# Seven block products with a PSUM tile each, and plain products for the first columns of each layer

## The chip, the cores and the metric

One core of a Trainium2 chip runs the whole program. The time is device microseconds (us) of one execution. Beside the timed executions one was taken by the hardware profiler; its trace is where all rows below come from.

## What is computed

Capped attention for 4 batches of 12 heads (448 rows, head size 64), then two feed-forward layers over the 1792 x 768 result, all in float32:

```python
scores = cap * np.tanh(scale * (q @ k.T) / cap)
attn = np.exp(scores - np.max(scores, axis=-1, keepdims=True))
x = (attn / (np.sum(attn, axis=-1, keepdims=True) + 1e-09)) @ v      # heads joined to 768 columns
h = np.maximum(x @ w_in, 0.0)          # layer 1: 768 -> 2048 -> 768
x = h * h @ w_out
g = x @ w_gate                         # layer 2: 768 -> 1536 -> 768
y = (g * (1.0 / (1.0 + np.exp(-g)))) * (x @ w_val) @ w_out2
```

## The kernel before

**Two passes.** Pass 0 computes the attention of batches 0 and 1, then the two layers for them, with the attention of batches 2 and 3 spread over its matmuls (12 pairs of heads, each opened by a gate at a certain matmul). Pass 1 computes the two layers for batches 2 and 3. Every float32 operand is split into two float32r parts, a high one (a cast on ScalarE) and a low one (a subtraction on VectorE), and a product is three matmuls (high x high, high x low, low x high) of 128 x 128 weights with 448 columns.

**Units of pass 1.** `pairs()` lists them: "1s" and "2s" are blocks that compute two columns of 128 of the hidden layer for both batches at once, "1b" and "2b" multiply the hidden layer by the second matrix in groups of FG = 4 columns (12 units of 12 matmuls in a group). A block takes two output columns, the two batches and the two halves of the 768 inputs as a 2 x 2 matrix of blocks and forms the product from seven block products instead of eight (the Strassen and Winograd scheme): 7 x 3 x 3 = 63 matmuls where plain ones need 72. There are 20 blocks: 8 in layer 1 (two ahead of each of its four groups), 12 in layer 2 (four ahead of each of its three).

**Operands of a block.** Four are the activations' quarters, named "11", "21", "12" and "22" (first digit: half of the inputs; second: batch 2 or 3), of three 128-row chunks c each. "12" is not an operand itself. Four sums T1 to T4 come from them (`SUMS`, `x_sum`, L579 to L582), and each operand is split by `o_hi` (ScalarE, L589) and `o_lo` (VectorE, L593). In layer 1 the quarters are read back from a DRAM copy, xhold (`x_back`, L572), in rounds by c, as their buffers have one or two places: T1 to T3 first (`BACK`), then again for "11", "21", "22" and T4 (`AGAIN`, which waits for the last T3). A last store into xhold follows the last attention pair's `norm` (L385). In layer 2 the quarters are the running sums of `gather` (L731).

**Products and PSUM.** `SEVEN` gives the seven products p0 to p6 in order; `s_mm` (L612) issues them. PSUM has eight places of 512 float32 columns: two for tag f0, two for f1, and a two-sided tile each for tags "s" and "a". p0 and p1 take f0, p4 takes f1; p2 and p3 are the two sides of one "s" tile, p5 and p6 the two sides of one "a" tile. `s_sum` reads them: p0 on ScalarE (L619), on VectorE u from p2 (L622), v from p3 (L625), w from p5 (L627), and the four results cs (L631) from p1, p4, p5 and p6. `unit_mm` (L682) issues all other products.

**Order.** The `Plan` class simulates the engines with fixed durations and writes one order for every engine from it; each step has a rank, which decides between steps that could start at the same time. AHEAD, LATER, FIRST, LAST, EARLIER and the like are parts of ranks or gates. Engines then work in that order; waits between engines follow from which tiles an instruction reads and writes.

Of the kernel before, what the change touches and what calls it, by code (L numbers as in the profile page):

```python
# [101 lines left out]
def kernel(  # L102
# [34 lines left out]
    FIRST = [15.0, 5]  # L137
    LAST = [80.7, 37.1]
    STRETCH = 2.1
    EARLIER = 16.02  # L140
    LEAD = 21.46
    BYC = 6.75
    BYK = 1.6

    AHEAD = dict(
        ld=28.6, lv=9.7, tr=8.5, cp=1.8, sc=9.4, th=-2.8, top=-8.4, par=14.9, mp=6.1, sub=21.2,
        ex=19.3, rs=-6.5, av=31.2, rc=15.1, norm=-38.3, xh=32.2, xl=26.8,
    )
# [4 lines left out]
    PACE = 7.11
    SLACK = 2.39
    MARGIN = 0.21
    DECODE = 77.14
# [402 lines left out]
    KINDS = ("11", "21", "T2", "T1", "22", "T3", "T4")  # L559
# [3 lines left out]
    for c in range(3):  # L563
        xo["11", c], xo["21", c], xo["T4", c], xo["22", c] = xbuf[0][c], xbuf[0][c + 3], xbuf[1][c], xbuf[1][c + 3]
# [26 lines left out]
    def o_lo(kind, c):  # L591
# [5 lines left out]
    SEVEN = ((0, 0, "11", "f0", 0), (0, 1, "21", "f0", 0), (2, 1, "T2", "s", 0), (2, 0, "T1", "s", 1),  # L597
             (3, 0, "22", "f1", 0), (1, 0, "T3", "a", 0), (1, 1, "T4", "a", 1))
    bank, u_t, c_t = {}, {}, {}

    def s_mm(i, p, c):
        k, half, kind, tag, side = SEVEN[p]
# [104 lines left out]
    def gate_m(i, b):  # L707
        sg = tmp_t[i, b] = fp.tile([P, S], F32, tag="sg", bufs=2, name="sg")
        V.scalar_tensor_tensor(sg, r_t.pop((i, b)), 1.0, ffn_ps.pop((i, b))[:, :S], ALU.add, ALU.mult)
# [124 lines left out]
    PAIR = 6.41  # L834
# [3 lines left out]
    for ps, (bs, seq) in enumerate(passes):  # L838
        order = [(i, b) for i, u in enumerate(seq) for b in bs[:: -1 if ps else 1] if b == bs[0] or not seven(u)]
        if ps == 0:  # L840
            order = [(i, b) for b in bs for i in range(NPRE)] + order[NPRE * len(bs) :]
        lens = [MM3 * (21 if seven(seq[i]) else cnt(seq[i])) for i, _ in order]
        heads, spent, at = 0, 0.0, t
        room = sum(lens) - FIRST[0] - LAST[0]
        late = B * KD - EARLY * KD
        for n, (i, b) in enumerate(order):
            if ps == 0 and heads < late and spent >= FIRST[0] + room * heads / (late - 1) - 1e-6:
                gates[EARLY * KD + heads] = steps[-1], t
                heads += 1
# [74 lines left out]
    def x_users(kind, c):  # L924
        return [("xt", 2, t, c) for t, two in SUMS.items() if kind in two] + [("xo", 2, kind, c)] * (kind in KINDS)
# [4 lines left out]
    for stage in (1, 2):  # L930
        for c in range(3):
            at = start_t[1, units7["12"[stage - 1]][0], 2] - 24 + BYC * c

            free_x = [("mm", 0, gone, b, x) for b in range(2) for x in (c, c + 3)]
            if stage == 1:
                for n, (kind, tag, bufs, to) in enumerate(BACK):
                    b, p = x_where(kind, c)
                    add(("xr", kind, c), "SP", (0.4, 0.6), at + n - EARLIER, x_back, (kind, c, tag, bufs),
                        [("hold", b * KD + p), ("norm", B * KD - 1)], [("rb" if tag == "r" else tag, bufs, [("xt", 1, t, c) for t in to])])
                for n, (kind, tag, bufs) in enumerate(AGAIN):  # L940
                    b, p = x_where(kind, c)
                    add(("xw", kind, c), "SP", (0.4, 0.6), at + n, x_back, (kind, c, tag, bufs), [("hold", b * KD + p), ("xt", 1, "T3", 2)],
                        [("rb" if tag == "r" else tag, bufs, [("xo", 1, kind, c)] + [("xt", 1, "T4", c)] * (kind == "21"))])
# [9 lines left out]
            for n, (kind, (one, two)) in enumerate(SUMS.items()):  # L953
                fourth = kind == "T4"
# [8 lines left out]
                add(("xt", stage, kind, c), "DVE", DVE1 * (1 + fourth), at + 4 + BYK * n - EARLIER * (stage == 1 and not fourth), summed, (kind, c), deps,  # L963
                    [("xt", 2, [("xo", stage, kind, c)] + [("xt", stage, "T2", c)] * (kind == "T1"))])
            for n, kind in enumerate(KINDS):
                ring = []
                if stage == 2:
                    deps = [src(kind), ("sm", last1, PART[kind], c)]
                elif (kind, c) in HOME:
                    deps = [src(kind)]  # L970
                    tag = HOME[kind, c]
                    ring = [(tag, RING[tag], [("sm", last2, PART[kind], 2)])]
                else:
                    deps = [src(kind) if kind in SUMS else ("xw", kind, c)] + free_x
# [5 lines left out]

                early = EARLIER * (stage == 1 and (kind, c) in HOME)
                add(("xi", stage, kind, c), "ACT", ACT1, at + 5 + BYK * n - early, high, (kind, c), deps, ring)
                add(("xo", stage, kind, c), "DVE", DVE1, at + 6 + BYK * n - early, o_lo, (kind, c), [("xi", stage, kind, c)])

    def plan_seven(i, t, prev):
# [3 lines left out]
        for p, (y, _, kind, tag, side) in enumerate(SEVEN):  # L989
            for c in range(3):  # L990
# [39 lines left out]
    for ps, (bs, seq) in enumerate(passes):  # L1030
        prev, before, when = None, {}, {}
        for ps_, i, b, t in [s for s in steps if s[0] == ps]:
# [5 lines left out]
            if ps and (i, b, 0) not in when:  # L1038
# [12 lines left out]
            for c in range(n):  # L1051
                deps = [("wl", ps, i)] if c == 0 else [K("mm", c - 1)] if ps == 0 else []
                if ps:
                    deps.append(before[i, b, c])
                if u[0] == "1a":
                    deps.append(("xl", b * KD + c))
# [6 lines left out]
                if c == 0 and u[0] == "1a" and not ahead:  # L1063
                    deps.append(("xl", b * KD + KD - 1))
# [11 lines left out]
            if ups(u):  # L1076
                used = [("mm", ps, m, b, u[1] % FG) for m, w in enumerate(seq) if not ups(w) and w[0][0] == u[0][0] and w[1] == u[1] // FG]
                G_ = ("g", GB, used)
# [5 lines left out]
            elif u[0] == "2a" and u[2] == 0:  # L1084
                add(K("gt"), "ACT", ACT1, end, gate_t, (i, b), [K("mm", n - 1)], [("r", 2, [K("gm")])])
                add(K("gm"), "DVE", DVE1, end + 0.5, gate_m, (i, b), [K("gt")], [("sg", 2, [("val", ps, i + 1, b)])])
# [5 lines left out]
            else:  # L1092
# [10 lines left out]
                add(K("ga"), "DVE" if g else "ACT", DVE1 if g else ACT1, end, gather, (i, b, e, g == 0), deps, ring)  # L1103
# [51 lines left out]
```

## Time and profile before

| | us |
|---|---|
| median of 3 runs | 1256.6 (1256.52 to 1257.73) |
| profiled execution, its own time | 1251.19 |
| its span, first to last instruction | 1249.1 |
| TensorE (PE) busy in the span | 1196.1 |
| VectorE (DVE) busy | 980.9 |
| ScalarE (ACT) busy | 577.6 |

The page of the profile gives busy times, the span in 40 slices with the granted clock of TensorE, the chain of work that ended last and the costliest groups of instructions. Matmuls overlap, so that their mean duration is longer than the distance between their starts, and a busy PE is not a PE at its peak.

### The profile page before, as it was taken

Reading aid. Unit: us, or ns where it says so; the run is one execution under the profiler, and the core shown is the slowest. Engines: PE = TensorE matmul, PEld = TensorE weight load, DVE = VectorE, ACT = ScalarE, POOL = GpSimd, SP = SyncE. Lnnn points to the kernel's source line nnn. Section 1 sums busy time; section 2 is a strip of 40 time slices with the busy share of each in tenths; the row PEclk is TensorE's granted clock in tenths of the full one; section 3 lists DMA queues with packets and bytes.
Section 4 is the critical chain, followed back from the end, with each engine's and each line's share of the span. In section 5 each row is a group of like instructions: output and inputs, shape, how many; then the busy total and the mean of one; then the engine's idle time right before and its main releaser. Section 6 shows DMA issues by size and latency. Waiting matters only on the chain.

```text
span 1249.1 us, 16273 instructions
## 1 busy us (share of the span) xinstructions
PE 1196.1 (96%) x6112; PEld 965.8 (77%) x6112; DVE 980.9 (79%) x1589; ACT 577.6 (46%) x886; POOL 73.3 (6%) x31
## 2 busy tenths in 40 slices
PE   8989999999999999999999979989899899999997
PEld 5334487887887887888788858878787798888887
DVE  5999888888888989888898987465646986576774
ACT  6998664635354343444224246452525444332330
POOL 2232110100000001010000000000000000000000
PEclk9999999999999999999999979999999899999999
DMA  7252068455554654744754754121212112111114
GB/s 139 68 135 67 16 170 225 113 152 165 153 142 126 170 162 126 217 128 131 191 150 135 201 154 125 53 68 40 64 33 68 50 35 81 49 54 64 43 34 89
DMA packets 215295, 136.93 MB, mean 110 GB/s; under 512 B 144912, under 2 KB 194224, under 8 KB 215216
## 3 DMA queue, kind: packets, MB, share of 16 engines
q1 hardware_dynamic: 213360, 135.66, 39.8%
q8 instruction: 48, 0.79, 0.3%
q10 hardware_dynamic: 1856, 0.23, 0.1%
q14 instruction: 31, 0.25, 0.1%
HBM read 100.86 MB, written 35.00 MB: 109 GB/s over the span
## 4 chain that ended last, share of the span: by engine, by line
PE 88%; DVE 8%; DMA 1%; issue 1%; ACT 1%; SPq 0%; POOL 0%; DVEq 0%
PE ff L682 55%; PE ff L612 21%; PE av L349 5%; PE sc L263 5%; DVE mx L282 1%; PE rs L313 1%; DVE te L300 1%; DVE cs L631 1%; DMA out_dram<-ob 1%; PE rs L333 0%; DVE acc L731 0%; DVE u L622 0%; DVE x L593 0%; DVE xt L582 0%; DVE u L627 0%
## 5 line engine op out<-in xcount | busy, mean ns | idle before, releaser
L682 PE MATMUL ff<-g,wp 128*128 128x448 f32 x2016 | 416.6, 367 | 2.9 <-DVE acc L731 2.1
L682 PEld LDWEIGHTS ff<-g,wp 128*128 128x128 f32 x2016 | 378.0, 188 | 42.9 <-issue 8.8
L682 PE MATMUL ff<-x,wp 128*128 128x448 f32 x1440 | 301.9, 368 | 0.0
L682 PEld LDWEIGHTS ff<-x,wp 128*128 128x128 f32 x1440 | 267.8, 188 | 41.4 <-issue 19.2
L612 PE MATMUL ff<-x,wp 128*128 128x448 f32 x720 | 165.3, 376 | 24.8 <-DVE cs L631 10.0
L612 PEld LDWEIGHTS ff<-x,wp 128*128 128x128 f32 x720 | 135.6, 192 | 46.8 <-DVE cs L631 15.3
L508 ACT CAST wp<-wx 128x512 fp32r<-128x512 f32 (+1 forms) x124 | 85.0, 687 | 124.3 <-DVE wx L490 79.3
L612 PE MATMUL ff<-xo,wp 128*128 128x448 f32 x540 | 120.6, 372 | 5.7 <-DVE u L622 5.7
L731 DVE TENSOR_TENSOR acc<-ff,acc 128x448 f32<-128x448 f32 x120 | 74.3, 622 | 59.1 <-PE ff L682 58.5
L612 PEld LDWEIGHTS ff<-xo,wp 128*128 128x128 f32 x540 | 102.7, 191 | 17.4 <-DVE u L622 8.7
L287 POOL PARTITION_ALL_REDUCE mr<-mx x24 | 72.5, 3023 | 587.0 <-DVE mx L282 544.1
L513 DVE TENSOR_TENSOR wp<-wx,wp 128x512 fp32r<-128x512 f32 (+1 forms) x124 | 95.8, 776 | 12.2 <-ACT wp L508 11.8
L263 PE MATMUL sc<-kT 64*112 64x448 f32 x384 | 86.9, 563 | 1.8 <-DVE kT L245 1.2
L631 DVE TENSOR_TENSOR cs<-ff,u 128x448 f32<-128x448 f32 x80 | 49.6, 621 | 37.2 <-PE ff L612 36.7
L304 ACT ACTIVATE tt<-tt,capt 112x896 f32<-112x896 f32 x60 | 62.4, 1046 | 21.5 <-DVE tt L300 21.4
L490 DVE SCALAR_TENSOR_TENSOR wx<-wr,wx 128x512 int32<-128x512 int32 (+1 forms) x82 | 68.2, 832 | 1.3
L488 DVE SCALAR_TENSOR_TENSOR wx<-wr,wx 128x512 int32<-128x512 int32 (+1 forms) x82 | 67.1, 818 | 1.6
L547 ACT CAST wp<-wx 128x768 fp32r<-128x768 f32 x40 | 33.4, 836 | 65.4 <-PE ff L682 46.3
L263 PEld LDWEIGHTS sc<-kT 64*112 64x112 f32 x384 | 30.5, 172 | 42.1 <-issue 25.8
L276 ACT ACTIVATE tt<-sc,capt 112x896 f32<-112x896 f32 x48 | 45.9, 1005 | 35.7 <-PE sc L263 35.6
L552 DVE TENSOR_TENSOR wp<-wx,wp 128x768 fp32r<-128x768 f32 x40 | 38.1, 953 | 25.2 <-ACT wp L547 25.1
L547 ACT CAST wp<-ws 128x384 fp32r<-128x384 f32 x60 | 29.0, 512 | 59.6 <-PE ff L612 30.2
(94 smaller groups left out, 1195.1 us busy)
## 6 DMA issues: line engine op xcount, KB each, us to landing
w<-wx SPq DMA_DIRECT2D x40, 384.0 KB, 2.8
wx<-w SPq DMA_DIRECT2D x40, 384.0 KB, 3.1
wr<-in_moe_w_in_dram SPq DMA_DIRECT2D x16, 768.0 KB, 5.7
wr<-in_moe_w_out_dram SPq DMA_DIRECT2D x24, 512.0 KB, 4.0
w<-wx SPq DMA_DIRECT2D x42, 256.0 KB, 2.3
wx<-w SPq DMA_DIRECT2D x42, 256.0 KB, 2.6
wr<-in_moe_w_gate_dram SPq DMA_DIRECT2D x12, 768.0 KB, 5.1
wr<-in_moe_w_val_dram SPq DMA_DIRECT2D x12, 768.0 KB, 5.3
```

Source lines behind the costliest of these rows:

```text
L263: PE.matmul(to, d["kT"][r, 0, c * CP : (c + 1) * CP], d["kT"][r, 1], start=True, stop=True)
L287: G.partition_all_reduce(d["m"].rearrange("p j s -> p (j s)"), d["mx"].rearrange("p j s -> p (j s)"), CP, bass_isa.ReduceOp.max)
L304: A.activation(t, t, AF.Exp, scale=c_abs)
L349: PE.matmul(d["av"][64 * j : 64 * j + 64, :S], d["v"][:, j, c], d["t", c][:, j], start=(c == 0), stop=(c == NC - 1),)
L488: V.scalar_tensor_tensor(x, hi, -0x40000000, x, ALU.bitwise_and, ALU.bitwise_or)
L490: V.scalar_tensor_tensor(x, lo, 29, x, ALU.logical_shift_right, ALU.bitwise_or)
L508: A.copy(piece((ps, i), n)[:, 0, :m], raws[1, i, i % 2] if ps else raws[0, i])
L513: V.tensor_tensor(hl[:, 1, :m], raws[1, i, i % 2] if ps else raws[0, i], f32(hl[:, 0, :m]), ALU.subtract)
L547: A.copy(t[:, 0, r], src)
L612: PE.matmul(bank[i, p], hl[:, h, 3 * half + c], x[:, t], start=(c == 0 and n == 0), stop=(c == 2 and n == 2))
L682: PE.matmul(ffn_ps[i, b][:, :S], hl[:, h, c], x[:, t], start=(c == 0 and s == 0), stop=(c == cnt(u) - 1 and s == 2),)
L731: V.tensor_tensor(acc, pt, acc, ALU.add)
```

## The change

Each of the seven products gets a PSUM tile of its own: p0 and p4 take f0, p1 and p5 f1, p2 the "s" tile, p3 and p6 the "a" tile one after the other. Of "s" and "a" only one side is then used. In layer 1 the first two hidden columns, in layer 2 the first (its gate and its value), are computed by plain products for both batches, ahead of the first block: 18 blocks are left. So "12" becomes an operand too, each quarter is read back once, T4 is built from the split parts of "21" and T2 and takes the place of "12" after the plain products. PSUM reads and gathers of pass 1 get ranks that are 7.08 us earlier (SOON), a plain gate's result lies in another buffer, and the constants of all ranks are new, those of the attention (AHEAD, LATER, LAST) included.

```diff
-    FIRST = [15.0, 5]
-    LAST = [80.7, 37.1]
+    FIRST = [14.9, 5]
+    LAST = [73.9, 48.9]
-    EARLIER = 16.02
+    EARLIER = 19.76
+    SOON = 7.08
+    LATE = 15.0
+    LATE1 = 3.26
...
     AHEAD = dict(
-        ld=28.6, lv=9.7, tr=8.5, cp=1.8, sc=9.4, th=-2.8, top=-8.4, par=14.9, mp=6.1, sub=21.2,
-        ex=19.3, rs=-6.5, av=31.2, rc=15.1, norm=-38.3, xh=32.2, xl=26.8,
+        ld=34.4, lv=38.5, tr=5.6, cp=7.5, sc=-0.1, th=-2.6, top=-8.2, par=19.2, mp=6.3, sub=20.7,
+        ex=23.5, rs=16.2, av=33.1, rc=15.5, norm=-54.6, xh=41.4, xl=27.7,
     )
     LATER = dict(
-        ld=-28.3, lv=13.1, tr=10.6, sc=1.2, th=13.5, top=1.1, par=3.7, sub=24.7, ex=-16.9,
-        tot=26.9, av=26.4, rc=11.3, norm=-43.0, xh=19.9, xl=21.8,
+        ld=-29.8, lv=13.4, tr=10.7, sc=2.1, th=7.4, top=-8.7, par=15.6, sub=24.6, ex=5.1,
+        tot=26.9, av=21.6, rc=22.1, norm=-52.8, xh=-6.6, xl=16.3,
     )
...
-                seq += [(n + "s", f) for f in range(FG * g, FG * g + FG, 2 // k2)]
+                cols = 0
+                if g == 0:
+                    cols = 2 // k2
+                    seq += [(n + "a", f, i) for f in range(cols) for i in range(k2)]
+                seq += [(n + "s", f) for f in range(FG * g + cols, FG * g + FG, 2 // k2)]
...
-    KINDS = ("11", "21", "T2", "T1", "22", "T3", "T4")
+    KINDS = ("11", "21", "12", "22", "T2", "T1", "T3", "T4")
...
-        xo["11", c], xo["21", c], xo["T4", c], xo["22", c] = xbuf[0][c], xbuf[0][c + 3], xbuf[1][c], xbuf[1][c + 3]
+        xo["11", c], xo["21", c], xo["12", c], xo["22", c] = xbuf[0][c], xbuf[0][c + 3], xbuf[1][c], xbuf[1][c + 3]
+        xo["T4", c] = xo["12", c]
...
-            V.tensor_tensor(t, xf[one, c], f32(xo[two, c][:, 0]), ALU.subtract)
-            V.tensor_tensor(t, t, f32(xo[two, c][:, 1]), ALU.subtract)
+            x, y = f32(xo[one, c]), f32(xo[two, c])
+            V.tensor_tensor(t, x[:, 0], y[:, 0], ALU.subtract)
+            V.tensor_tensor(t, t, x[:, 1], ALU.add)
+            V.tensor_tensor(t, t, y[:, 1], ALU.subtract)
...
-    SEVEN = ((0, 0, "11", "f0", 0), (0, 1, "21", "f0", 0), (2, 1, "T2", "s", 0), (2, 0, "T1", "s", 1),
-             (3, 0, "22", "f1", 0), (1, 0, "T3", "a", 0), (1, 1, "T4", "a", 1))
+    SEVEN = ((0, 0, "11", "f0"), (0, 1, "21", "f1"), (2, 1, "T2", "s"), (2, 0, "T1", "a"),
+             (3, 0, "22", "f0"), (1, 0, "T3", "f1"), (1, 1, "T4", "a"))
...
-                if side == 0:
-                    bank[i, tag] = (ps_s if tag == "s" else ps_a).tile([P, 2, 512], F32, tag=tag, name="ff")
-                bank[i, p] = bank[i, tag][:, side, :S]
+                bank[i, p] = (ps_s if tag == "s" else ps_a).tile([P, 2, 512], F32, tag=tag, name="ff")[:, 0, :S]
...
-    BACK = (("12", "xs", 2, ("T1", "T3")), ("11", "r", 1, ("T1",)), ("22", "v", 2, ("T2", "T3")))
-    AGAIN = (("11", "r", 1), ("21", "xs", 2), ("22", "v", 2))
+    BACK = (("11", "r", 1), ("21", "xs", 2), ("12", "xs", 2), ("22", "v", 2))
...
-                deps = [("xw", one, c) if fourth and stage == 1 else src(one), ("xo", stage, two, c) if fourth else src(two)]
+                if kind == "T4":
+                    deps = [("xo", stage, one, c), ("xo", stage, two, c)] + [("mm", 1, i, 3, c) for i in plain]
+                else:
+                    deps = [src(one), src(two)]
...
-                if c == 0 and side == 0:
-                    rel = {0: [("sp1", i)], 1: [("s11", i)], 2: [("su", i), ("sv", i)], 4: [("s12", i)], 5: [("s22", i), ("sw", i), ("s21", i)]}[p]
-                    ring = [(tag, 2 if tag in ("f0", "f1") else 1, rel)]
+                if c == 0:
+                    rel = {0: ["sp1"], 1: ["s11"], 2: ["su"], 3: ["sv"], 4: ["s12"], 5: ["s22", "sw"], 6: ["s21"]}[p]
+                    ring = [(tag, 2 if tag in ("f0", "f1") else 1, [(x, i) for x in rel])]
...
-        at = lambda p: t + 3 * MM3 * (p + 1)
+        at = lambda p: t + 3 * MM3 * (p + 1) - SOON
...
+            if ps and ups(u):
+                for x in [(i, b, c) for c in range(n)]:
+                    before[x], when[x] = prev, t + MM3 * x[2]
+                    prev = ("mm", 1, *x)
...
-                add(K("ga"), "DVE" if g else "ACT", DVE1 if g else ACT1, end, gather, (i, b, e, g == 0), deps, ring)
+                add(K("ga"), "DVE" if g else "ACT", DVE1 if g else ACT1, end - SOON * ps, gather, (i, b, e, g == 0), deps, ring)
```

## Rows read from the trace of the kernel before

**Rows 1.** The page: busy time (share) x instructions of each engine.
```profile
PE 1196.1 (96%) x6112; PEld 965.8 (77%) x6112; DVE 980.9 (79%) x1589; ACT 577.6 (46%) x886; POOL 73.3 (6%) x31
```

**Rows 2.** Windows: us, busy (x count) of PE, PEld, DVE, ACT, POOL, clock, DMA, GB/s.
```profile
37.00:107.00 70.00, 62.84 (x446) 24.71 (x435) 67.55 (x105) 63.42 (x85) 19.08 (x6) 1.00 0.43 104
157.00:700.00 543.00, 543.00 (x2706) 444.87 (x2706) 468.22 (x714) 238.46 (x345) 35.96 (x12) 1.00 0.57 156
```

**Rows 3.** Waits of PE over the whole span: us in total, times, longest.
```profile
PE ff L612 <- DVE cs L631: 10.0, 14, 0.7
PE ff L612 <- ACT x L589: 7.8, 4, 3.7
PE ff L612 <- DVE u L622: 5.7, 8, 0.7
PE rs L313 <- ACT te L304: 5.2, 5, 2.4
PE ff L612 <- DVE u L627: 4.3, 6, 0.7
```

**Rows 4.** Chain that ended last, a stall of layer 1: start, us, what.
```profile
809.06 0.64 DVE u L622
...
809.74 5.15 PE ff L612 x24
```

**Rows 5.** Timeline, a block in which p2 and p3 run without a stall.
```profile
1076.63 3.81 PE L612 MATMUL ff<-xo,wp 128*128 128x448 f32 x18
1080.27 1.99 PE L612 MATMUL ff<-x,wp 128*128 128x448 f32 x9
...
1080.47 0.62 DVE L622 TENSOR_TENSOR u<-ff,u 128x448 f32<-128x448 f32 x1 [1.48 <-PE ff L612]
```

**Rows 6.** Chain that ended last: runs of blocks (L612) and of second products (L682).
```profile
862.97 6.70 PE ff L612 x33
...
894.39 29.18 PE ff L682 x144
...
1073.14 11.56 PE ff L612 x57
...
1129.40 29.20 PE ff L682 x144
1158.61 24.33 PE ff L612 x120
...
1213.60 29.20 PE ff L682 x144
```

**Rows 7.** Timeline, from pass 0 to pass 1.
```profile
701.74 0.62 DVE L385 TENSOR_TENSOR xs<-av,rb 128x448 f32<-128x448 f32 x1
701.94 19.61 PE L682 MATMUL ff<-g,wp 128*128 128x448 f32 x96
...
774.30 0.88 PE L682 MATMUL ff<-g,wp 128*128 128x448 f32 x3 [0.31 <-DVE g L661]
```

**Rows 8.** Windows as in rows 2, on the way into layer 1.
```profile
702.00:745.00 43.00, 33.76 (x139) 28.19 (x138) 39.23 (x72) 15.91 (x29) 0.00 (x0) 0.84 0.68 190
738.00:740.00 2.00, 0.57 (x1) 0.29 (x1) 2.00 (x5) 0.60 (x2) 0.00 (x0) 0.50 0.61 237
```

**Rows 9.** DMA issues from 700 to 741: count, KB each, us to landing.
```profile
xr<-xhold SPq DMA_DIRECT2D x18, 224.0 KB, 3.4
```

**Rows 10.** Timeline of PE and a window, from layer 1 to layer 2.
```profile
954.96 29.35 PE L682 MATMUL ff<-g,wp 128*128 128x448 f32 x144
990.90 0.72 PE L612 MATMUL ff<-x,wp 128*128 128x448 f32 x1 [1.63 <-ACT x L589]
...
985.00:999.00 14.00, 10.66 (x36) 8.44 (x35) 13.97 (x27) 6.11 (x12) 0.00 (x0) 0.76 0.17 48
```

**Rows 11.** Window, as in rows 2: an inner block of layer 2.
```profile
1087.00:1101.00 14.00, 13.28 (x66) 11.96 (x65) 12.15 (x22) 6.67 (x12) 0.00 (x0) 1.00 0.14 39
```

**Rows 12.** Costliest groups on DVE, 702 to 745: busy, mean ns, idle before.
```profile
L593 DVE TENSOR_TENSOR x<-xr,x 128x448 fp32r<-128x448 f32 x8 | 4.8, 617 | 0.5 <-ACT x L589 0.5
```

More of the change, by code (lines that the diff above doesn't have):

```diff
@@ L136 @@
     GB, TBUF, WP, NPRE, NWARM = 10, 4, 4, 3, 30
-    FIRST = [15.0, 5]
-    LAST = [80.7, 37.1]
+    FIRST = [14.9, 5]
+    LAST = [73.9, 48.9]
     STRETCH = 2.1
-    EARLIER = 16.02
+    EARLIER = 19.76
+    SOON = 7.08
+    LATE = 15.0
+    LATE1 = 3.26
     LEAD = 21.46
-    BYC = 6.75
-    BYK = 1.6
+    BYC = 6.06
+    BYK = 0.74
     AHEAD = dict(
-        ld=28.6, lv=9.7, tr=8.5, cp=1.8, sc=9.4, th=-2.8, top=-8.4, par=14.9, mp=6.1, sub=21.2,
-        ex=19.3, rs=-6.5, av=31.2, rc=15.1, norm=-38.3, xh=32.2, xl=26.8,
+        ld=34.4, lv=38.5, tr=5.6, cp=7.5, sc=-0.1, th=-2.6, top=-8.2, par=19.2, mp=6.3, sub=20.7,
+        ex=23.5, rs=16.2, av=33.1, rc=15.5, norm=-54.6, xh=41.4, xl=27.7,
     )
     LATER = dict(
-        ld=-28.3, lv=13.1, tr=10.6, sc=1.2, th=13.5, top=1.1, par=3.7, sub=24.7, ex=-16.9,
-        tot=26.9, av=26.4, rc=11.3, norm=-43.0, xh=19.9, xl=21.8,
-    )
[L153 to L156, printed above, removed]
+        ld=-29.8, lv=13.4, tr=10.7, sc=2.1, th=7.4, top=-8.7, par=15.6, sub=24.6, ex=5.1,
+        tot=26.9, av=21.6, rc=22.1, norm=-52.8, xh=-6.6, xl=16.3,
+    )
+    PACE = 7.04
+    SLACK = 2.38
+    MARGIN = 0.25
+    DECODE = 79.0
     const = ctx.enter_context(tc.tile_pool(name="const", bufs=1))
@@ L593, in o_lo @@
         V.tensor_tensor(t[:, 1], xf[kind, c], f32(t[:, 0]), ALU.subtract)
-    SEVEN = ((0, 0, "11", "f0", 0), (0, 1, "21", "f0", 0), (2, 1, "T2", "s", 0), (2, 0, "T1", "s", 1),
-             (3, 0, "22", "f1", 0), (1, 0, "T3", "a", 0), (1, 1, "T4", "a", 1))
+    SEVEN = ((0, 0, "11", "f0"), (0, 1, "21", "f1"), (2, 1, "T2", "s"), (2, 0, "T1", "a"),
+             (3, 0, "22", "f0"), (1, 0, "T3", "f1"), (1, 1, "T4", "a"))
     bank, u_t, c_t = {}, {}, {}
     def s_mm(i, p, c):
-        k, half, kind, tag, side = SEVEN[p]
+        k, half, kind, tag = SEVEN[p]
         if c == 0:
@@ L707, in gate_m @@
     def gate_m(i, b):
-        sg = tmp_t[i, b] = fp.tile([P, S], F32, tag="sg", bufs=2, name="sg")
+        if b < 2:
+            sg = tmp_t[i, b] = fp.tile([P, S], F32, tag="sg", bufs=2, name="sg")
+        else:
+            sg = tmp_t[i, b] = ap.tile([P, S], F32, tag="xs", bufs=2, name="sg")
         V.scalar_tensor_tensor(sg, r_t.pop((i, b)), 1.0, ffn_ps.pop((i, b))[:, :S], ALU.add, ALU.mult)
@@ L830, in plan_pair @@
             add(K("xl"), "DVE", DVE1, R("xl"), x_lo, (b, p, s), [K("xh")])
-    PAIR = 6.41
+    PAIR = 6.6
     steps = []
@@ L838 @@
     for ps, (bs, seq) in enumerate(passes):
-        order = [(i, b) for i, u in enumerate(seq) for b in bs[:: -1 if ps else 1] if b == bs[0] or not seven(u)]
+        order = [(i, b) for i, u in enumerate(seq) for b in bs[:: -1 if ps and not ups(u) else 1] if b == bs[0] or not seven(u)]
         if ps == 0:
@@ L922, with x_users @@
     gone = max(i for i, u in enumerate(passes[0][1]) if u[0] == "2a")
-    def x_users(kind, c):
-        return [("xt", 2, t, c) for t, two in SUMS.items() if kind in two] + [("xo", 2, kind, c)] * (kind in KINDS)
-    BACK = (("12", "xs", 2, ("T1", "T3")), ("11", "r", 1, ("T1",)), ("22", "v", 2, ("T2", "T3")))
-    AGAIN = (("11", "r", 1), ("21", "xs", 2), ("22", "v", 2))
+    def x_users(stage, kind, c):
+        return [("xt", stage, t, c) for t, two in SUMS.items() if t != "T4" and kind in two] + [("xo", stage, kind, c)]
+    BACK = (("11", "r", 1), ("21", "xs", 2), ("12", "xs", 2), ("22", "v", 2))
+    PART["12"] = PART["T4"]
     last1, last2 = units7["1"][-1], units7["2"][-1]
     for stage in (1, 2):
+        plain = [i for i, u in enumerate(passes[1][1]) if u[0] == f"{stage}a"]
         for c in range(3):
-            at = start_t[1, units7["12"[stage - 1]][0], 2] - 24 + BYC * c
+            at = start_t[1, plain[0], 2] - EARLIER + BYC * c
             free_x = [("mm", 0, gone, b, x) for b in range(2) for x in (c, c + 3)]
             if stage == 1:
-                for n, (kind, tag, bufs, to) in enumerate(BACK):
+                for n, (kind, tag, bufs) in enumerate(BACK):
                     b, p = x_where(kind, c)
[L938 to L943, printed above, removed]
+                    add(("xr", kind, c), "SP", (0.4, 0.6), at - 10 + n, x_back, (kind, c, tag, bufs),
+                        [("hold", b * KD + p), ("norm", B * KD - 1)], [("rb" if tag == "r" else tag, bufs, x_users(1, kind, c))])
             def src(x):
@@ L953 @@
             for n, (kind, (one, two)) in enumerate(SUMS.items()):
-                fourth = kind == "T4"
-                deps = [("xw", one, c) if fourth and stage == 1 else src(one), ("xo", stage, two, c) if fourth else src(two)]
+                if kind == "T4":
+                    deps = [("xo", stage, one, c), ("xo", stage, two, c)] + [("mm", 1, i, 3, c) for i in plain]
+                else:
+                    deps = [src(one), src(two)]
                 def summed(kind, c, stage=stage):
@@ L961, in summed @@
                     x_sum(kind, c)
-                add(("xt", stage, kind, c), "DVE", DVE1 * (1 + fourth), at + 4 + BYK * n - EARLIER * (stage == 1 and not fourth), summed, (kind, c), deps,
+                add(("xt", stage, kind, c), "DVE", DVE1 * (3 if kind == "T4" else 1), at + (LATE if stage == 2 else LATE1) + BYK * n, summed, (kind, c), deps,
                     [("xt", 2, [("xo", stage, kind, c)] + [("xt", stage, "T2", c)] * (kind == "T1"))])
@@ L966 @@
                 ring = []
+                deps = [src(kind)]
                 if stage == 2:
-                    deps = [src(kind), ("sm", last1, PART[kind], c)]
+                    deps.append(("sm", last1, PART[kind], c))
                 elif (kind, c) in HOME:
-                    deps = [src(kind)]
                     tag = HOME[kind, c]
@@ L973 @@
                 else:
-                    deps = [src(kind) if kind in SUMS else ("xw", kind, c)] + free_x
+                    deps += free_x
                 def high(kind, c, stage=stage):
@@ L979, in high @@
                     o_hi(kind, c)
-                early = EARLIER * (stage == 1 and (kind, c) in HOME)
-                add(("xi", stage, kind, c), "ACT", ACT1, at + 5 + BYK * n - early, high, (kind, c), deps, ring)
-                add(("xo", stage, kind, c), "DVE", DVE1, at + 6 + BYK * n - early, o_lo, (kind, c), [("xi", stage, kind, c)])
+                when_ = at + ((LATE if stage == 2 else LATE1) + BYK * (n - 4) if kind in SUMS else n)
+                add(("xi", stage, kind, c), "ACT", ACT1, when_ + 1, high, (kind, c), deps, ring)
+                add(("xo", stage, kind, c), "DVE", DVE1, when_ + 2, o_lo, (kind, c), [("xi", stage, kind, c)])
     def plan_seven(i, t, prev):
@@ L988, in plan_seven @@
         f = u[1]
-        for p, (y, _, kind, tag, side) in enumerate(SEVEN):
+        for p, (y, _, kind, tag) in enumerate(SEVEN):
             for c in range(3):
@@ L1036 @@
                 continue
-            if ps and (i, b, 0) not in when:
+            if ps and ups(u):
+                for x in [(i, b, c) for c in range(n)]:
+                    before[x], when[x] = prev, t + MM3 * x[2]
+                    prev = ("mm", 1, *x)
+            elif ps and (i, b, 0) not in when:
                 one = [x for x in range(i, i + KD)]
@@ L1052 @@
                 deps = [("wl", ps, i)] if c == 0 else [K("mm", c - 1)] if ps == 0 else []
-                if ps:
+                if ps and before[i, b, c]:
                     deps.append(before[i, b, c])
                 if u[0] == "1a":
-                    deps.append(("xl", b * KD + c))
+                    deps.append(("xo", 1, f"{1 + c // 3}{b - 1}", c % 3) if ps else ("xl", b * KD + c))
+                elif u[0] == "2a" and ps:
+                    deps.append(("xo", 2, f"{1 + c // 3}{b - 1}", c % 3))
                 elif u[0] == "2a":
@@ L1062 @@
                 ahead = ps == 0 and b == 1 and i < NPRE
-                if c == 0 and u[0] == "1a" and not ahead:
+                if c == 0 and u[0] == "1a" and not ahead and ps == 0:
                     deps.append(("xl", b * KD + KD - 1))
@@ L1076 @@
             if ups(u):
-                used = [("mm", ps, m, b, u[1] % FG) for m, w in enumerate(seq) if not ups(w) and w[0][0] == u[0][0] and w[1] == u[1] // FG]
+                used = [("mm", ps, m, b, u[1] % FG) for m, w in enumerate(seq) if w[0] == u[0][0] + "b" and w[1] == u[1] // FG]
                 G_ = ("g", GB, used)
@@ L1085 @@
                 add(K("gt"), "ACT", ACT1, end, gate_t, (i, b), [K("mm", n - 1)], [("r", 2, [K("gm")])])
-                add(K("gm"), "DVE", DVE1, end + 0.5, gate_m, (i, b), [K("gt")], [("sg", 2, [("val", ps, i + 1, b)])])
+                add(K("gm"), "DVE", DVE1, end + 0.5, gate_m, (i, b), [K("gt")], [("xs" if ps else "sg", 2, [("val", ps, i + 1, b)])])
             elif u[0] == "2a":
@@ L1098 @@
                     ring = [(f"acc{b % 2}", 3, [y for x in (e, e + 1) for y in ([("otr", b, x)] if L == "2" else [("yl", b, x)] if ps == 0
-                             else x_users(f"{1 + x // 3}{b - 1}", x % 3))])]
+                             else x_users(2, f"{1 + x // 3}{b - 1}", x % 3))])]
                 deps = [done] + ([("ga", ps, seq.index((u[0], g - 1, e)), b)] if g else [])
```

## The prediction

> **What bounds the kernel now.** I read the page first: TensorE (PE) is busy 96% of the span [rows 1], so the end is set by how densely its matmuls follow one another. Busy time does not show that, since matmuls overlap, so I measured the distance between starts: 144 second products in a row take 29.18 us [rows 6], 0.2026 us a matmul, where nothing holds PE up. At that pitch a block of 63 takes 12.77 us. Then I looked for the stretches that fall short of it. From 157 to 700 us PE has no gap (543.0 of 543.0) [rows 2], and its waits as a list [rows 3] lie almost all in pass 1 or in the first 157 us. So pass 1 holds what can be gained, and the chain of waits and the timeline show three losses there.
>
> First, inside the blocks. PE waits for the VectorE (DVE) reads of PSUM, cs, u (L622) and w (L627), 14 + 8 + 6 = 28 times, 20.0 us in all [rows 3]. In the chain PE stands still exactly as long as u takes and goes on 0.04 us after it [rows 4]. Yet u reads p2, and the matmuls that wait are those of p3, which shares p2's tile and has no use for u. Likewise cs and w read p5 while p6, in the same tile, waits. Where u comes only after p3 has ended, p2 and p3 run as 18 matmuls without a stall [rows 5]. So the waits come from sharing a tile. Their true price is read from the runs between second products [rows 6]: two blocks of layer 1 take 894.39 - 862.97 = 31.42 us where 126 x 0.2026 = 25.53 are needed: 5.9 lost with six waits, and there are three such pairs. Four blocks of layer 2 take 56.26 and 54.99 us where 51.06 are needed: 5.2 with five waits and 3.9 with four. With the one wait left over at 1.0 this is 17.7 + 5.2 + 3.9 + 1.0 = 27.8 us, 0.99 a wait, more than the 0.72 of idle time, because the pipeline has to fill again.
>
> Second, the way into layer 1. From 701.94 to 774.30 us PE issues the last 144 matmuls of pass 0, two blocks and 7 more, 277 in all [rows 7]: 56.1 us at full pitch, 72.4 measured, 16.2 lost. PE waits there for operands being split (ACT x, longest 3.7 us [rows 3]), DVE is busy 39.2 of 43 us, and after the stalls the granted clock is 0.50 (1.2 GHz) [rows 8], so part of the loss is slow matmuls. Third, the way into layer 2: 144 matmuls from 954.96 and four blocks should end at 1035.2; the next 144 begin 29.2 before the run at 1073.14, at 1044.0. That is 8.8 lost, of which 1.0 is counted above: 7.8. DVE is busy 13.97 of 14 us there [rows 10]. Together 27.8 + 16.2 + 7.8 = 51.8 us.
>
> **The change part by part.** *A tile for each product.* All 28 waits lose their cause: -27.8. New waits come with the new places. p6 takes the only place of "a" after p3, so it waits until v (L625) has read p3. Between the end of p3 and the start of p6 lie p4 and p5, 18 x 0.2026 = 3.6 us, and v needs 0.62 after u. Behind a waiting p6 stand all of PE's later matmuls, and behind v on DVE's queue nothing that frees it sooner. p3 of the next block waits for the cs of p6, three products earlier; f0 and f1 turn over once a block, which is as long. All of these hold if DVE is prompt. An inner block of layer 2 has 12.15 us of DVE in 14 [rows 11]; compressed to 12.77 that is 95%, so it is not prompt everywhere. No row shows p6 waiting for v. Below, zero; above, half the old loss, 13.9. I keep 3.0, near zero, because 3.6 us is several DVE steps of 0.62 and the earlier ranks put these reads ahead.
>
> *Plain products.* 72 matmuls take the place of 63 in each layer: 18 x 0.2026 = +3.65 us on PE, all on the path. In return, the sums are first needed 72 + 18 matmuls (p0, p1) after the quarters: 18 us later. On DVE each layer gains three third steps of T4 and three o_lo of "12", 6 x 0.617 = 3.7 us [rows 12], and loses a block's seven PSUM reads (4.3 us) and seven short weight steps (at most 4.3): between 0.6 and 5 us less. The read-backs of layer 1 go from 18 to 12 (3.4 us to landing each [rows 9]) and from six rounds to three, on SP's queue among the output stores and the weight reads, which move up by as much.
>
> *Way into layer 1.* Pass 0's 144 matmuls, the plain 72 and p0, p1 give 234 x 0.2026 = 47.4 us of PE work before a sum is needed, against 39.2 us of DVE work in the 43 us up to that point now [rows 8], plus 1.9 for the low parts of "12". So DVE fits. The reads decide: they need the last norm, which lies at 701.74 [rows 7], and LAST opens the last attention pair up to 6.8 us of matmuls later: 709. Now the six rounds fill the time from 702 to 741, 6.5 each, so three rounds and a split end near 730. The products of pass 0 end at 731, and the last chunks are wanted between 732 and 738. That just fits, with DVE full of pass 0's gathers and transposes. Kept loss: none at best, today's 16.2 at worst. I take 6.0, nearer to zero by the rounds above, since a slip of 2 us can bring the 0.50 clock with it.
>
> *Way into layer 2.* The last running sum ends with the matmuls of layer 1, but its chunk is the sixth that the first plain unit wants, 15 matmuls = 3.0 us later, against three steps of 0.6 each. T4 must now come after the plain products have left its place, 14 us before p6 needs it. Kept: 2.0, between 0 and 7.8, nearer zero since the saturated 14 us now have 14.6 us of plain products over them.
>
> *New ranks of the attention.* They add no work and move its order. From 157 us on, PE has no gap to lose; in 37 to 107 us PE is busy 62.8 of 70 with DVE at 67.6 [rows 2], so order can give or take a few us. I take 0, bounds -4 and +4. The plain gate's other buffer costs nothing: it is free between blocks; were it not, DVE would wait for one value step of 0.62 us.
>
> **Sum.** -27.8 - 16.2 - 7.8 + 3.0 + 6.0 + 2.0 + 3.65 = -37.2 us. From the profiled execution's 1251.2 (span 1249.1 and 2.1 around it) that gives 1214.0. The median of the runs lies 5.4 us above that execution, and I carry this over: 1219.5.
>
> **Rivals.** *DVE becomes the bound inside the blocks.* For it: 95% in inner blocks [rows 11]. Against it: the read of a second product's result comes long before its place is wanted. If v costs p6 0.75 us in each of 18 blocks, 13.5 stays in place of 3.0: 1230.
>
> *The transitions stay.* For it: DVE saturated in both [rows 8, 10], and the last norm later. Against it: three rounds for six, and 14.6 us of cover. Both old losses kept, 24.0 in place of 8.0: 1235.5.
>
> *The split does nothing.* The waits could come from something else than the shared tile, such as DVE's reads having to stand apart from matmuls anyway. Then 26.8 of them stay, and only the transitions are won: -16.2 - 7.8 + 8.0 + 3.65 = -12.4, 1244. Against it: rows 5, and that all 28 fall on p3 and p6. The Trainium skill, in "PSUM — Partial Sum Buffer" (PSUM bank collisions raise a hardware error), says that PSUM must be guarded by bank and 32-partition quadrant, a bank being 512 float32 columns. The two sides of the old tile are two such banks, so by that rule a read of one needs no wait on the other's matmuls and the two-sided tile was not the cause: this rival's time. The trace speaks against that reading, since the waits are there, though no row says who put them.
>
> *Slower.* The new ranks hold PE up in each of the 12 attention pairs that pass 0 carries. PE has no gap there now and DVE is 86% busy [rows 2], and the exponential moves back in LATER by 22 ranks. The nearest price is the early pairs' wait for ACT te, 5.2 us in five times, longest 2.4 [rows 3]. It decides from 37.2 / 12 = 3.1 us a pair; at 4 us it gives 48 - 37.2, 1267. Against it: PE has other matmuls to run at any time in that stretch.
>
> **How the numbers follow.** Forecast 0.68, DVE as the bound 0.11, transitions stay 0.11, no effect of the split 0.04, slower 0.06. With all kept terms at zero the time is 1208.5; the first three cases end at 1235.5, and I add 2.5 for the ranks: 1208 to 1238. These hold 0.90, and I leave 0.08 of that for their tails. A measurement of this kernel can tell about 0.2% (2.5 us) from no change. Faster by more 0.91; within it 0.03, where the split does nothing and a transition gets worse; slower 0.06.
>
> **What would show it.** Right: no wait of L612 for L622, L627 or cs; runs of two blocks in 25.5 to 27 us and of four in 51 to 53; from the last norm's 144 matmuls to the first block a granted clock of 1.00 and stalls below 6 us. A list of waits with p6 behind u (L625) speaks for the first rival, one with ACT x for the second, waits for cs unchanged for the third, and waits in 157 to 700 for the last. The prediction is wrong if the chain through PE in pass 1 no longer sets the end, or if those 543 us grow.

## The result, and the profile after

| | before | after |
|---|---|---|
| median of 4 runs, us | 1256.56 (1254.84 to 1257.73) | 1212.89 (1205.43 to 1217.11) |
| profiled execution, its own time | 1251.19 | 1205.43 |
| its span | 1249.1 | 1203.7 |

The ratio is 0.9647 (95% interval 0.9598 to 0.9696): 43.7 us faster by the medians, 45.4 by the spans. A second set of four runs of the changed kernel gave 1207.09 (1203.90 to 1216.68), 0.9618 (0.9571 to 0.9665) of the kernel before. Executions of the changed kernel lie up to 13 us apart, those of the kernel before up to 7, so among variants of the changed kernel a difference of some us is read from the traces and not from the medians. Part of that spread is the start of the dense part of pass 0, its first run of 144 second products in the chain that ended last. In the kernel before, and then in the changed one:

```profile
175.83 29.38 PE ff L682 x144
```

```profile
177.38 29.38 PE ff L691 x144
```

In the eleven traces of this document it starts anywhere from 175.8 to 180.6 us, with the old ranks of the attention (175.8, 176.3, 179.9) as with the new ones. From this start to the end of the span the kernel before takes 1073.3 us and the changed kernel 1026.3 and 1026.4 in its two traces, 47 us less. Below, "from the dense start" means this count; it compares single executions without that part of the spread.

The page of the profile after, busy time as in rows 1:

```profile
PE 1183.7 (98%) x6130; PEld 967.6 (80%) x6130; DVE 972.6 (81%) x1573; ACT 573.1 (48%) x884; POOL 73.5 (6%) x31
```

18 matmuls more, and yet PE counts as busy 12.4 us less. At least a part of this is that a matmul counted longer where the clock had fallen: 139 of them 33.76 us in rows 8, 0.243 us each. All waits of PE in the changed kernel of 0.5 us or more in total, as in rows 3:

```profile
PE rs L316 <- ACT te L307: 5.5, 6, 2.4
PE tr L229 <- ACT te L279: 3.9, 4, 2.0
PE sc L266 <- DVE kT L248: 1.2, 1, 1.2
PE warm L764 <- DVE zero L1136: 1.0, 1, 1.0
PE ff L691 <- DVE x L604: 0.6, 1, 0.6
```

L621 now issues the block products, L691 the plain ones. No wait of L621 is left; of pass 1 only the last row remains. The others lie in the first 157 us and were there before. The chain that ended last, as in rows 6 (the first pieces at the way into layer 1):

```profile
734.91 13.44 PE ff L691 x65
748.35 12.77 PE ff L621 x63
761.11 29.29 PE ff L691 x144
790.40 25.54 PE ff L621 x126
815.93 29.18 PE ff L691 x144
...
925.38 43.77 PE ff L691 x216
969.15 38.30 PE ff L621 x189
1007.45 29.18 PE ff L691 x144
1036.64 51.07 PE ff L621 x252
1087.71 29.18 PE ff L691 x144
1116.89 51.07 PE ff L621 x252
```

Two blocks take 25.54 us (31.42 before), four take 51.07 (56.26 and 54.99), at the full pitch of 0.2026 us a matmul. The way into layer 2 is one dense piece: 144 second products and 72 plain ones in 43.77 us, then three blocks. Only at the way into layer 1 is something left:

```profile
706.94 0.62 DVE L388 TENSOR_TENSOR xs<-av,rb 128x448 f32<-128x448 f32 x1
...
734.91 13.44 PE L691 MATMUL ff<-x,wp 128*128 128x448 f32 x65 [0.61 <-DVE x L604]
```

(timeline), and the window over it, columns as in rows 2:

```profile
702.00:749.00 47.00, 46.38 (x232) 40.72 (x229) 42.81 (x81) 22.03 (x41) 0.00 (x0) 1.00 0.57 166
```

The last norm stands 5.2 us later than in rows 7; DVE is as busy as in rows 8, 42.8 of 47 us, but PE now has work to run meanwhile and the granted clock stays at 1.00.

### The profile page after: what moved, and what is told of

The parts are those of the page before. It is cut to its first block, busy times and chain, and to the rows that moved or that the text cites. A ratio compares the mean times of both kernels' runs of the same rounds, so it can differ in the third digit from the quotient of the medians.

```text
span 1203.7 us, 16287 instructions
## 1 busy us (share of the span) xinstructions
PE 1183.7 (98%) x6130; PEld 967.6 (80%) x6130; DVE 972.6 (81%) x1573; ACT 573.1 (48%) x884; POOL 73.5 (6%) x31
## 4 chain that ended last, share of the span: by engine, by line
PE 94%; ACT 2%; DMA 1%; DVE 1%; issue 0%; SPq 0%; POOL 0%; ACTq 0%; DVEq 0%
PE ff L691 60%; PE ff L621 19%; PE av L352 6%; PE sc L266 6%; PE rs L316 2%; ACT te L307 1%; ACT te L279 1%; PE rs L336 1%; ACT tt L277 0%; PE tr L229 0%; DMA wx<-w 0%; DMA xr<-xhold 0%; DMA out_dram<-ob 0%; DVE mx L285 0%; DMA kq<-in_q_dram 0%
## 5 line engine op out<-in xcount | busy, mean ns | idle before, releaser
L691 PE MATMUL ff<-g,wp 128*128 128x448 f32 x2016 | 414.7, 366 | 0.0
L691 PEld LDWEIGHTS ff<-g,wp 128*128 128x128 f32 x2016 | 377.5, 188 | 39.3 <-issue 9.5
L691 PE MATMUL ff<-x,wp 128*128 128x448 f32 x1584 | 331.8, 368 | 0.6 <-DVE x L604 0.6
L691 PEld LDWEIGHTS ff<-x,wp 128*128 128x128 f32 x1584 | 294.8, 188 | 44.6 <-issue 18.9
L516 ACT CAST wp<-wx 128x512 fp32r<-128x512 f32 (+1 forms) x128 | 88.3, 693 | 129.8 <-DVE wx L498 72.3
L621 PE MATMUL ff<-x,wp 128*128 128x448 f32 x648 | 138.3, 365 | 0.0
L621 PEld LDWEIGHTS ff<-x,wp 128*128 128x128 f32 x648 | 121.7, 188 | 9.6
L521 DVE TENSOR_TENSOR wp<-wx,wp 128x512 fp32r<-128x512 f32 (+1 forms) x128 | 99.5, 782 | 8.3 <-ACT wp L516 7.5
L621 PE MATMUL ff<-xo,wp 128*128 128x448 f32 x486 | 104.3, 365 | 0.0
L621 PEld LDWEIGHTS ff<-xo,wp 128*128 128x128 f32 x486 | 91.3, 188 | 7.2
L640 DVE TENSOR_TENSOR cs<-ff,u 128x448 f32<-128x448 f32 x72 | 44.8, 622 | 23.2 <-PE ff L621 22.0
L555 ACT CAST wp<-wx 128x768 fp32r<-128x768 f32 x36 | 30.1, 836 | 64.5 <-PE ff L691 40.6
L733 DVE TENSOR_TENSOR g<-gg,g 128x448 fp32r<-128x448 f32 x62 | 39.9, 646 | 20.1 <-ACT g L729 20.0
L729 ACT CAST g<-gg 128x448 fp32r<-128x448 f32 x62 | 35.1, 566 | 41.5 <-DVE gg L725 39.3
```

The source lines that it names most:

```text
L516: A.copy(piece((ps, i), n)[:, 0, :m], raws[1, i, i % 2] if ps else raws[0, i])
L521: V.tensor_tensor(hl[:, 1, :m], raws[1, i, i % 2] if ps else raws[0, i], f32(hl[:, 0, :m]), ALU.subtract)
L691: PE.matmul(ffn_ps[i, b][:, :S], hl[:, h, c], x[:, t], start=(c == 0 and s == 0), stop=(c == cnt(u) - 1 and s == 2),)
```

## The experiments

**Only the tiles.** The kernel before with this part of the change alone (the table; the allocation of the tiles and their releases follow from it):

```diff
-    SEVEN = ((0, 0, "11", "f0", 0), (0, 1, "21", "f0", 0), (2, 1, "T2", "s", 0), (2, 0, "T1", "s", 1),
-             (3, 0, "22", "f1", 0), (1, 0, "T3", "a", 0), (1, 1, "T4", "a", 1))
+    SEVEN = ((0, 0, "11", "f0"), (0, 1, "21", "f1"), (2, 1, "T2", "s"), (2, 0, "T1", "a"),
+             (3, 0, "22", "f0"), (1, 0, "T3", "f1"), (1, 1, "T4", "a"))
```

> The kernel before with one part of the change: the seven products get a PSUM tile each and their releases; no plain products, all ranks as before. My theory (the 28 waits come from the shared tile): no wait of a block product for u or cs is left, the runs of two and four blocks take 25.5 and 51 us, the two transitions lose their 16 and 8 us as before: 1229 us (1227 to 1234). Rival, the split does nothing: 1256. Rival, DVE becomes the bound inside the blocks: the waits for cs and u are replaced by waits for v, 1240.

Measured: 1237.92 us (1236.52 to 1241.71), 0.9855 (0.9827 to 0.9884). Waits of PE (L610 issues the block products, L623 is v):

```profile
PE ff L610 <- ACT x L589: 9.3, 4, 4.0
...
PE ff L610 <- DVE u L623: 5.1, 1, 5.1
```

Two runs of blocks from the chain that ended last, of two blocks and of four:

```profile
813.35 26.04 PE ff L610 x126
...
1067.63 51.07 PE ff L610 x252
```

All waits for u, cs and w are gone: the shared tile was their cause. Yet 9 us of the expected gain are missing from the median, 13 from the span (1234.5, where 1249.1 - 27.8 = 1221.3 was due), and the trace shows where. One block, the first of layer 1, has the new wait that the prediction named: p6 waits 5.1 us for v. Runs of two blocks take 26.04 and not 25.54 us, a slower pitch without any wait (last section), some 4 us in all. And this execution was 4 us later at the start of the dense part of pass 0, in which the two kernels do not differ. The late v in the timeline:

```profile
766.27 0.62 DVE L623 TENSOR_TENSOR u<-ff,u 128x448 f32<-128x448 f32 x1
```

p3 had ended at 758.2. DVE is not full there: from 757 to 767 us it is busy 8.2 of 10 us. But u, which v needs, starts only at 765.21, behind weight steps and two transposes for the output, the first of which waits 1.6 us for an output store. So the place of the reads in DVE's order made v late; the earlier ranks of the change are left out here.

**The pairs back.** The changed kernel with the same edit undone, the plain products and ranks kept.

> The changed kernel with that part undone: p2 and p3, p5 and p6 share a two-sided tile again, p0 and p1 take f0; plain products and new ranks stay. My theory: the waits come back in 18 blocks, at least 1.25 a block as before (23 waits, 23 us), at most three a block, since the reads now have earlier ranks (54 waits, 53 us): 1236 to 1266 us, transitions still without loss. Rival, the gain came from the plain products and the ranks: 1213.

Measured: 1241.28 us (1240.86 to 1241.77), 0.9878 (0.9851 to 0.9906). Its waits (L642 is cs, L633 u from p2, L638 w):

```profile
PE ff L623 <- DVE cs L642: 10.0, 14, 0.7
PE ff L623 <- DVE u L633: 8.6, 12, 0.7
PE ff L623 <- DVE u L638: 4.3, 6, 0.7
```

32 waits in 18 blocks, each 0.7 us of idle time. The span is 32.1 us over that of the changed kernel's second execution, 1207.0, whose dense start is within 0.7 us of the same time: 1.0 us a wait, the price that the prediction took from rows 6 (0.99). By the medians the edit is worth 19.5 us in the kernel before and 28 to 34 in the changed one.

**Plain products in layer 1 only.** The changed kernel with

```diff
-                if g == 0:
+                if g == 0 and n in PLAIN:          # PLAIN = "1"
```

and the ranks of layer 2's sums counted from its first block; the operand "12" is left out there.

> The changed kernel without the plain products of layer 2: its first column is a block again, with 9 matmuls less, and the sums of layer 2 are needed at once. My theory (the plain products cover the splitting and summing of the operands): 1.8 us less of matmuls, and up to the 7.8 us of the old transition come back: 1217 to 1220 us, PE waiting for operands (ACT x, DVE x) at the start of layer 2, DVE full there. Rival, the transition was cured by the other order of the sums: 1211, no such waits.

Measured: 1220.37 us (1215.0 to 1222.82), 0.9705 (0.967 to 0.974). The longest of its waits in pass 1, two for a sum:

```profile
PE ff L622 <- ACT xo L601: 7.5, 2, 6.1
```

A window at the start of layer 2, columns as in rows 2:

```profile
956.00:972.00 16.00, 7.40 (x30) 5.25 (x28) 15.64 (x29) 6.58 (x12) 0.00 (x0) 0.74 0.17 50
```

p2 waits for its sum, DVE is busy 15.6 of 16 us and the clock falls. From the chain, the 144 matmuls before and the four blocks take 93.8 us where 80.2 are needed: 13.6 lost, 0.6 of that by the slower pitch. The plain products' 1.8 us buy some 13. That is more than the 7.8 of the kernel before; probably these ranks, made for a layer that begins with plain products, put the sums late, but no run separates this.

**The changed kernel once more**, on the chip of the three runs above.

> The changed kernel once more, on the same chip as the three others: 1205 to 1217 us as before, PE in pass 1 with less than 2 us of waits. If the time is above 1212, its trace shows where the difference to the execution of 1205.4 us lies: my guess is the way into layer 1, where the read-backs land just ahead of their use.

Measured: 1207.09 us, the profiled execution 1208.69 with a span of 1207.0. The guess was wrong: the way into layer 1 is the same to the tenth (one wait of 0.6 us). The 3.3 us lie in the first part: the dense start is at 180.57 instead of 177.38, and from there the two executions agree to 0.1 us.

**Plain products in layer 2 only.** PLAIN = "2", and SOON = 3.0.

> The changed kernel without the plain products of layer 1 (its first two columns are a block again, 9 matmuls less), with SOON = 3 in place of 7.08, since the planner finds no order otherwise. My theory (the plain products cover the reads, splits and sums): 1.8 us less of matmuls and 10 to 16 us of the old transition come back: 1218 to 1230 us, PE waiting for ACT x, xo and DVE x between 735 and 765 us, the granted clock at 0.50 for some of it. Rival, three rounds of reads in place of six cured it: 1207 to 1212, no such waits.

Measured: 1229.57 us (1224.6 to 1234.09), 0.9803 (0.9771 to 0.9835). Its longest waits from 157 us on:

```profile
PE ff L692 <- DVE acc L744: 10.4, 1, 10.4
PE ff L622 <- DVE u L635: 3.3, 1, 3.3
```

A window on the way into layer 1, columns as in rows 2:

```profile
722.00:745.00 23.00, 12.26 (x52) 10.60 (x51) 21.82 (x40) 9.14 (x16) 0.00 (x0) 0.78 0.52 153
```

The old loss is back, with three rounds of reads in place of six: from 705.08 to 776.92 us PE issues 261 matmuls, 52.9 us at full pitch, so 18.9 are lost, where the kernel before lost 16.2. So at these ranks the shorter rounds alone do not cure it. SOON differs too, but without any SOON (below) the changed kernel loses 4.4 us and not 19. PE is held by a running sum that stands late on the full DVE, not by the operands that I had named, and p6 waits for v as in the first experiment. From the dense start the execution takes 1050.9 us, 24.6 more than the changed kernel; the slower pitch, from 777 us to the end of this execution, is 8.8 of that (last section). The median is 17 us above the changed kernel's first set.

**The old ranks of the attention.** AHEAD, LATER, FIRST, LAST, PACE, SLACK, DECODE and PAIR as before, all else as changed.

> The changed kernel with the constants of the attention and its gates as before: AHEAD, LATER, FIRST, LAST, PACE, SLACK, DECODE and PAIR; tiles, plain products and the ranks of pass 1 stay. My theory (the new order of the attention is worth nothing by itself): 1205 to 1217 us, the last norm some 5 us earlier against the end of pass 0, so the way into layer 1 no worse, and no gap of PE from 157 us on. Rival, the ranks of the attention carry a part of the gain (an earlier start of pass 0 or the way into layer 1): 1218 to 1226, with PE waits there.

Measured: 1212.75 us (1212.28 to 1213.25), 0.9671 (0.9652 to 0.969). The median does not tell it from the changed kernel. The list of waits from 157 us on does, with its only row:

```profile
PE ff L691 <- ACT x L600: 4.9, 1, 4.9
```

The 216 matmuls between 702.37 and the first block end at 754.1 where 746.1 would do: 8.0 us lost on the way into layer 1, against 1.0. From the dense start the execution takes 1033.6 us, 7.3 more than the changed kernel. So the ranks do carry some 7 us there, in the one execution traced; I had given them nothing. The last norm came at 702.2, 4.8 us earlier than in the changed kernel, and the stall all the same: an earlier norm does not prevent it. Which of the ranks prevents it was not tested.

**No earlier ranks for the reads.** SOON = 0.0.

> The changed kernel with SOON = 0: the reads of PSUM and the gathers of pass 1 get no earlier ranks. My theory (3.6 us between p3 and p6 are enough for v at any rank): less than 3 us slower, 1207 to 1220, at most a few waits for v. Rival, DVE is late without the ranks: waits for v, cs or acc of 0.5 us or more in most of the 18 blocks, 1222 to 1232.

Measured: 1213.16 us (1210.41 to 1215.67), 0.9673 (0.9648 to 0.9697). The one wait of a block product:

```profile
PE ff L621 <- DVE u L634: 1.9, 1, 1.9
```

It is p6 waiting for v in the first block of layer 1. Behind it the granted clock is 0.57 (763.3 to 767.0 us). From the dense start the execution takes 1030.7 us, 4.4 more than the changed kernel: more than the 3 that I had expected, most of it at that block. In the other 17 blocks v comes in time without the earlier ranks.

**How late v may be.** The read of p3 four and seven times over, with the same result:

```diff
-            V.tensor_tensor(u_t[i, "v"], bank[i, 3], u_t[i, "u"], ALU.add)
+            for _ in range(4):                      # 7 in the second kernel
+                V.tensor_tensor(u_t[i, "v"], bank[i, 3], u_t[i, "u"], ALU.add)
```

> The changed kernel with v computed four times over in each of the 18 blocks (three more DVE steps of 0.53 to 0.62 us, same result): v is done 1.6 us later and DVE has 1.6 us more in a block of 12.8. My theory: v ends 2.6 us ahead of p6 in an inner block, so p6 does not wait for v itself, but DVE falls behind where it is 95% busy: 2 to 10 us slower, 1210 to 1224. Rival, DVE is at its edge in every block: 18 x 1.6 = 29 us slower, 1236 to 1244.

Measured: 1212.78 us (1210.58 to 1216.66), 0.9673 (0.9649 to 0.9697); the median does not tell it from the changed kernel. An inner block of layer 2 in the timeline of the changed kernel (L634 is v; the 27 matmuls begin with p6), and then in this one (L635 is v):

```profile
1056.93 0.62 DVE L634 TENSOR_TENSOR u<-ff,u 128x448 f32<-128x448 f32 x1
...
1060.19 5.63 PE L621 MATMUL ff<-x,wp 128*128 128x448 f32 x27
```

```profile
1060.64 2.59 DVE L635 TENSOR_TENSOR u<-ff,u 128x448 f32<-128x448 f32 x4
...
1063.28 3.98 PE L621 MATMUL ff<-x,wp 128*128 128x448 f32 x18
```

A window over the next 13 us of it, columns as in rows 2:

```profile
1065.00:1078.00 13.00, 13.00 (x63) 11.54 (x63) 12.86 (x24) 6.49 (x12) 0.00 (x0) 1.00 0.12 40
```

In the changed kernel v ends 2.64 us before p6 starts. With three steps more it starts 0.6 us nearer to p6, takes 2.0 longer and ends 0.05 us before it: in this block the slack is used up to the last. DVE is busy 12.86 of 13 us there (11.95 from 1050 to 1063 us in the changed kernel), and the run of four blocks around it takes 51.67 us instead of 51.07, without a wait. Over the whole kernel the steps are not free: from the dense start this execution takes 1032.1 us, 5.7 more than the changed kernel, inside the 2 to 10 that I had expected. The first three blocks of layer 2 alone take 39.9 us where 38.3 are needed; three waits for v are 1.7 us in all, two shorter waits 0.5, and a part lies in stretches at the slower pitch (last section), among them the last 144 matmuls in 29.89 us.

> As the run with v computed four times over, but seven times: v is done 3.2 us later and DVE has 3.2 us more in a block of 12.8, 15.3 in an inner block of layer 2 where 12.1 stand now. With four times over, v ended just as p6 was due in an inner block and DVE was busy 12.8 of 13. My theory (that was the edge, from here DVE sets the pace inside the blocks): about 1.6 us a block in 18 blocks, 20 to 35 us slower, 1232 to 1247, waits for v in most blocks. Rival, DVE still has room in the stretches between blocks and catches up: under 10 us, below 1222.

Measured: 1249.84 us (1248.24 to 1251.26), 0.9958 (0.9941 to 0.9976), 37 us above the changed kernel. Its longest wait from 157 us on:

```profile
PE ff L621 <- DVE u L635: 27.9, 18, 3.2
```

An inner block in the timeline:

```profile
1069.67 4.58 DVE L635 TENSOR_TENSOR u<-ff,u 128x448 f32<-128x448 f32 x7 [0.49 <-PE ff L621]
...
1074.30 2.90 PE L621 MATMUL ff<-x,wp 128*128 128x448 f32 x13 [1.02 <-DVE u L635]
```

A window in layer 1, columns as in rows 2:

```profile
790.00:816.00 26.00, 24.98 (x123) 22.84 (x123) 16.17 (x28) 13.87 (x26) 0.00 (x0) 1.00 0.15 49
```

All 18 blocks wait for v, those of layer 1 too, where DVE is busy 16.2 of 26 us. DVE starts on v at once, but seven reads take 4.58 us and p6 follows p3 by 3.65. So the delay from p3 to p6 decides, not DVE's load: 1.55 us of idle time a block. From the dense start this execution takes 1068.9 us, 42.6 more than the changed kernel; the 14.7 us beyond the 27.9 are 0.8 a stall. The granted clock falls here too (0.989 over the span, 0.997 in the changed kernel).

## Why the prediction was right

The sum was -37.2 us and the spans show -45.4; 1219.5 was forecast and 1212.9 measured. The mechanisms were right, three kept terms were too large, and the new ranks did something that the sum had at nothing. The number itself lies nearer to the edge than to the middle: 1212.9 is 4.9 us above the lower end of the range, and the second set of the same kernel, 1207.1, is 0.9 below it.

- *The waits inside the blocks*, -27.8: shown by both experiments on the tiles, and by the runs of blocks at full pitch. Reading the price from the runs (0.99 a wait) and not from the idle time (0.72) was right: 1.0 came back with the pairs.
- *New waits*, 3.0 kept: nothing was lost. The mechanism is real, as the seven-fold v shows, and so is the rival *DVE becomes the bound*, but its edge is 2.6 us of delay away in an inner block. My 95% of load was the wrong measure. The rival's price also appeared in the first block of layer 1, where v came late in DVE's order: a wait of 5.1 us where the tiles came alone, and 1.9 us without the earlier ranks. So that nothing was lost there rests on these ranks.
- *Plain products*, +3.65: 18 matmuls at full pitch in the chain, as worked out.
- *Way into layer 1*, 6.0 kept: 1.0 was lost (207 matmuls from 705.25 to 748.19 us, 42.9 us where 41.9 are needed). The estimate that the last split would end near 730 was 9 us early: the reads took 4.5 us to land instead of 3.4 and stood behind output stores, and the split ended at 739.3, 1 us ahead of its matmul. That so little was lost with an estimate so far off was in part luck. What the step had right is the cover: without the plain products the loss is back, with the reads in three rounds.
- *Way into layer 2*, 2.0 kept: nothing was lost (405 matmuls in 82.07 us, 82.05 needed). Without the plain products some 13 are.
- *Ranks of the attention*, 0 within 4: the dense start is 1.5 us later than before in the one execution and 4.7 in the other, which is within what it moves by with either set of ranks, so nothing was gained there. But they carry some 7 us on the way into layer 1, more than the bound of 4, and a part that the prediction had placed with the plain products and the shorter rounds alone.

Summed from the two traces: -27.8 - 15.2 - 7.8 + 3.65 + 1.5 = -45.7, against -45.4; from the dense start, without the 1.5, -47.2 against -47.0. The sum was thus 8.6 us short for the profiled execution; the median stood 7.5 us above that one and not 5.4, which leaves 6.6.

Of the other rivals, *the split does nothing* fell with the first experiment. The Trainium skill (PSUM — Partial Sum Buffer, section PSUM bank collisions raise a hardware error) asks for PSUM to be guarded by bank and quadrant. That is not contradicted here: the two sides are two banks, and in the changed kernel reads of one bank run beside matmuls into another without a wait. The tile experiments show that sharing the tile brings the waits; that the program put them there, by ordering accesses to a tile as a whole, is the likely reading and was not shown by itself. *The transitions stay* is what leaving out the plain products of one layer gives, for the way into that layer. *Slower* needed gaps of PE after 157 us in pass 0; there are none (543.0 us busy of the 543.0 to 700).

## What to carry to other kernels

If a reader of one half of a tile and a writer of the other half alternate, each has to wait for the other although they touch nothing in common; look for waits exactly as long as one read, and price them by the length of the whole run. A full engine says little by itself: in inner blocks DVE at 92% of the time cost nothing and at 99% 0.6 us in four blocks, and at 62% it cost 1.5 us a block when one result came too late. Measure the slack of the step that somebody waits for, and where executions scatter, count from a point behind the scatter: only so did the 5.7 us of the longer v show. Work that needs no sums or late operands, put ahead of work that does, can be worth several times its price at a change of stage.

## What was not expected of the hardware

The same stream of matmuls has two pitches at the same granted clock. In the execution without layer 2's plain products the chain that ended last shows both:

```profile
815.33 29.76 PE ff L692 x144
...
1020.70 29.19 PE ff L692 x144
```

and the windows give a clock of 1.00 (the third number from the end) for either stretch:

```profile
815.00:845.00 30.00, 30.00 (x147) 27.25 (x146) 17.47 (x30) 7.02 (x12) 0.00 (x0) 1.00 0.18 64
...
1020.00:1049.00 29.00, 29.00 (x145) 26.89 (x144) 12.55 (x22) 10.96 (x20) 0.00 (x0) 1.00 0.20 61
```

0.2067 and 0.2026 us a matmul, 2% apart, with nothing waiting. The slower one began at 760 us here and ended with the stall at the start of layer 2; in another execution it lasted from 777 us to the end, about 8.8 us over 2151 matmuls. Both traces of the changed kernel have the faster one almost throughout. Together with a dense start that moves by up to 4.7 us, it is of the size of the spread between executions of one kernel; that it is their cause was not shown, and what sets the pitch stays open.
